# k and q turned by VectorE instead of TensorE in a pack attention with a softplus FFN behind it

## The chip, the cores and the metric

The kernel runs on one core of one Trainium2 chip. A core has five engines with instruction streams of their own: TensorE (PE in the profile; its weight loads are listed as PEld), VectorE (DVE), ScalarE (ACT), GpSimd (POOL) and SyncE (SP), whose queue issues nearly all DMAs here. The metric is the device time of one execution in microseconds: 802.89 us as the median of 3 runs, 802.77 to 803.67.

## What is computed

Eight batches of eight heads, 576 tokens, head size 64. Each head has 32 pack queries p. First the packs attend to the tokens, then the tokens attend to the packs, and the heads side by side (512 wide) go through a feed-forward layer of width 2048 with softplus. The weights of that layer come as 64-bit floats.

```
p_packed = softmax(p @ k.T / 8) @ v             # per batch and head: 32 x 64
a        = softmax(q @ p_packed.T / 8) @ p_packed   # 576 x 64
x        = heads of a side by side              # 4608 x 512
h        = x @ w_in                             # 4608 x 2048
out      = softplus(h) @ w_out                  # 4608 x 512
```

## The kernel before

**Groups and orientation.** The heads form two groups g of four (`HG`). For scores, the contraction over the head size has to lie on partitions, so k and q are needed turned: head size down, tokens across. `load` (L112) brings four heads of k, q or v as a tile of 96 partitions by 4 heads by 6 tokens by 64: each partition reads runs of six tokens, 1536 bytes. `transposed` (L223) turns one head: three TensorE transposes (L228) into a PSUM bank, two tokens of a run each, so that 128 partitions hold even tokens in the upper half and odd tokens in the lower, and one ScalarE copy (L234) to SBUF, the tile `T`. `scores1` and `scores2` (L241) multiply from there. The second scores are turned back by VectorE 32x32 transposes (L308, L332), which move data by blocks of 32 without TensorE.

The last attention product, by p_packed, is not computed as such: `make_m` (L447, bank `psm`) multiplies p_packed by a column chunk of w_in, and gemm1 takes the attention weights `at_h`, `at_l` against that.

**The FFN, in units.** A unit is one block of 128 of the 2048 columns for one batch, 16 units a batch. `gemm1` (L484) is twelve matmuls into two banks `ph` (a pool of two), three for each product since both sides are split into a high and a low part. The softplus is Abs, Exp and Ln on ScalarE (L506, L508, L509) into `e` and a max-and-add on VectorE (L511); POOL copies a rest of 64 tokens aside (L515), and VectorE splits `e` into `gh` and `gl` (L498, L499). `gemm2` (L522) of the unit two before follows: four tiles of 128 tokens, three matmuls each, into four banks `acc` that live through a batch. After an odd batch a fifth tile `acc_m` gathers the rests. `store` (L529) copies each result and writes it out.

**Stages.** In stage b the units of batch b run, and beside them, in steps of a generator, `attention` of batch b+1: a pacing number (`PACE`) says how many of its steps go between two gemm2 tiles. `make_m` stands behind the gemm2 of unit u for the chunk that starts at unit u+2: a chunk is 256 columns in batch 0, so every even unit has one, and 512 later. Stage 0 also runs `convert` (L148), another generator, paced by `CONV`: 32 pieces of the 64-bit weights, in the order i0 i1 o0 o1 i2 i3 o2 o3 and so on (i a block of w_in, o one of w_out). A piece is loaded into an `x` tile (L131), read twice by ScalarE (`m`, L173, and `r`, L177), worked on twice by VectorE (L179, L184) and added by POOL (L192), for i into `w_in_sb`; for o ScalarE and VectorE make `wo_h` (L211) and `wo_l` (L217) of it. From the ninth piece on there are two `x` tiles, so a load waits until the piece two before has been read.

**What sets the order.** TensorE's order is the order of the program text (`manual_schedule`). The orders of ScalarE, VectorE, POOL and SP are laid out when the kernel is built, by a scheduler that goes by its own idea of durations; on the chip they are fixed, and each engine runs its rows in order.

Of the kernel before, what the change touches and what calls it, by code (L numbers as in the profile page):

```python
# [9 lines left out]
F32 = mybir.dt.float32  # L10
# [16 lines left out]
def pack_attention_then_softplus_ffn(  # L27
# [10 lines left out]
    nc = tc.nc  # L38
    B, H, S, D = q.shape
    J = p.shape[2]  # L40
# [11 lines left out]
    LAG = 2  # L52
    MC = 512
    scale = 1.0 / math.sqrt(D)
# [23 lines left out]

    BG = P // J
    pT = const.tile([P, H, P], F32, name="pT")  # L80

# [10 lines left out]
    def load_pack(bg, queues):  # L92

        t = cv.tile([P, H, D], F32, tag="m", name=f"p_{bg}", bufs=1)
        for i in range(BG):
            queues[i % len(queues)].dma_start(
                t[i * J:(i + 1) * J], p[bg * BG + i].rearrange("h j d -> j h d")
            )
        return t

    def pack_transposed(bg, t):
        for o in range(0, H, HG):
            ps = bank(f"ppt_{bg}_{o}")
            for i in range(HG):
                nc.tensor.transpose(ps[:D, i * P:(i + 1) * P], t[:, o + i, :], ident)  # L105
            dst = pT[:, o:o + HG, :].rearrange("x h j -> x (h j)")
            nc.vector.tensor_copy(dst[:D], ps[:D])
            nc.scalar.copy(dst[D:], ps[:D])

    loaded = {}  # L110

    def load(nm, b, g):  # L112
        if b >= B:
            return
        t = ld.tile([NP, HG, SI, D], F32, tag="ld", name=f"{nm}_{b}_{g}")
        nc.sync.dma_start(
            t.rearrange("x h s d -> x h (s d)"),
            {"q": q, "k": k, "v": v}[nm][b, g * HG:(g + 1) * HG].rearrange(
                "h (x s) d -> x h (s d)", s=SI
            ),  # L120
        )
        loaded[nm, b, g] = t
# [99 lines left out]

    def transposed(nm, b, g, hh):  # L223

        src = loaded[nm, b, g]
        ps = bank(f"psT_{nm}_{b}_{g}_{hh}")
        for i in range(HS):
            nc.tensor.transpose(  # L228
                ps[:, i * NP:(i + 1) * NP],
                src[:, hh, 2 * i:2 * i + 2, :].rearrange("x s d -> x (s d)"),  # L230
                ident[:NP, :NP],
            )
        dst = work.tile([P, C], F32, tag="T", name=f"T_{nm}_{b}_{g}_{hh}", bufs=4)
        nc.scalar.copy(dst, ps[:, :C])  # L234
        return dst
# [98 lines left out]

    def attention(b):


        a1 = [work.tile([P, S], F32, tag="a1", name=f"a1_{b}_{g}") for g in range(G)]
        pp = [None] * G
        kT, qT = [], []  # L340
        for hh in range(HG):
            kT.append(transposed("k", b, 0, hh))
            yield
        load("q", b, 0)
# [4 lines left out]
        kT = [transposed("k", b, 1, 0)]  # L349
        yield  # L350
        z0 = softmax1_exp(b, 0, a1[0], nm)
        kT.append(transposed("k", b, 1, 1))
        yield
        rs0 = softmax1_sum(b, 0, z0)
        for hh in range(2, HG):
            kT.append(transposed("k", b, 1, hh))
            yield
        load("q", b, 1)
        for c in range(2):
# [12 lines left out]
        yield  # L372
        qT.append(transposed("q", b, 0, 0))
        yield
# [5 lines left out]
        yield  # L380
        qT.append(transposed("q", b, 0, 1))
        yield
# [3 lines left out]
        for hh in range(2, HG):  # L386
            qT.append(transposed("q", b, 0, hh))
            yield
# [28 lines left out]
        softmax2_div(b, 1, 1, a2n)  # L417
        yield

    def weights(b):  # L420
# [105 lines left out]

    outv = [out[b * S:(b + 1) * S, :].rearrange("(x s) e -> s x e", s=SI) for b in range(B)]

    def store(acc, pieces, nm):  # L529
        o = cv.tile([P, DM], F32, tag="x", name=f"o_{nm}", bufs=2)  # L530
        nc.vector.tensor_copy(o, acc)  # L531
        for row, b, col, n in pieces:
            while n:
                i, x = divmod(col, NP)
                m = min(n, NP - x)
                s = i % HS * 2 + i // HS
                nc.sync.dma_start(outv[b][s, x:x + m, :], o[row:row + m, :])
                row, col, n = row + m, col + m, n - m
# [142 lines left out]
```

## Time and profile before

| | |
|---|---|
| median of 3 runs | 802.89 us (802.77 to 803.67) |
| profiled execution | 803.84 us |
| its span, first to last instruction | 802.0 us |
| mean granted TensorE clock | 0.981 |
| packets under 512 bytes | 4864 of 38215 |
| k, q, v loads | 16 each, 576 KB, 4.6 to 4.8 us to landing |
| start of gemm1 in stages 0, 1, 2 | 44.9 (held to 49.5), 157.1, 243.3 us |

A row of a group gives the line, the engine, the operation, output and input tiles with shapes and a count; then the busy time in us, the mean of one in ns, and the idle time before such instructions with what ended it. A row by stretches gives the stretch, its length, then busy time and count of PE, PEld, VectorE, ScalarE and POOL, the granted clock, the DMA share and GB/s. A row of the timeline gives start, duration, engine, line and operation, and in brackets a wait and what ended it.

### The profile page before, as it was taken

To read this page: it belongs to the slowest core of one execution; us is meant where nothing else is said; L and a number is where in the kernel's file an instruction comes from. 1 tells how busy PE (TensorE), PEld (TensorE's weight loads), DVE (VectorE), ACT (ScalarE), POOL (GpSimd) and SP (SyncE) were. 2 spreads that over 40 slices of the span, in tenths; PEclk is the share of its full clock that TensorE was granted. 3 is DMA by queue.
4 is the path that set the end of the run, shared out by engine and by line. 5 is a ranking of instruction groups with operands and counts; after the bars stand their busy time and mean duration, and the time that the engine had idled before them with its cause. 6 is when DMAs were issued, how large, how long until landed. Compare 5 with 4: busy or idle time off the path is not lost.

```text
span 802.0 us, 14807 instructions
## 1 busy us (share of the span) xinstructions
PE 762.9 (95%) x5632; PEld 602.1 (75%) x5632; DVE 512.1 (64%) x1168; ACT 465.0 (58%) x1181; POOL 93.8 (12%) x166
## 2 busy tenths in 40 slices
PE   6368998999999999999999999999999999999997
PEld 4246666787788787887888777878778777878886
DVE  2787869864677447764677446765587546764554
ACT  5658877666554555675555465566556355555540
POOL 1414443100000000000000000000000000000010
PEclk9957999999999999999999999999999999999999
DMA  9975866022212112132212122122210210010002
GB/s 234 244 166 144 208 175 160 14 83 60 60 30 83 26 48 60 31 83 60 60 30 52 45 61 60 31 83 61 60 31 24 73 31 1 1 51 3 1 1 66
DMA packets 38215, 56.00 MB, mean 70 GB/s; under 512 B 4864, under 2 KB 31488, under 8 KB 38144
## 3 DMA queue, kind: packets, MB, share of 16 engines
q1 hardware_dynamic: 37600, 54.93, 26.7%
q8 instruction: 44, 0.72, 0.4%
q14 instruction: 27, 0.22, 0.1%
q10 hardware_dynamic: 544, 0.13, 0.1%
HBM read 45.61 MB, written 9.44 MB: 69 GB/s over the span
## 4 chain that ended last, share of the span: by engine, by line
PE 79%; ACT 0%; DVE 0%; issue 0%; ACTq 0%; DVEq 0%
PE acc L522 40%; PE ph L484 23%; PE acc_m L522 5%; PE psm L447 3%; PE ps L241 2%; PE psT_q L228 1%; PE psT_k L228 1%; PE psp L284 1%; PE psa L274 1%; PE psx L297 0%; PE ppt L105 0%; ACT e L509 0%; ACT e L508 0%; ACT e L506 0%; DVE o L531 0%; DVE o_m L531 0%
## 5 line engine op out<-in xcount | busy, mean ns | idle before, releaser
L511 DVE SCALAR_TENSOR_TENSOR e<-ph,e 128x288 f32<-128x288 f32 x256 | 114.5, 454 | 173.2 <-ACT e L509 170.2
L522 PE MATMUL acc<-wo_h,gh 128*128 128x512 f32 x512 | 214.5, 419 | 0.7 <-DVE o L531 0.7
L522 PE MATMUL acc<-wo_h,gl 128*128 128x512 f32 x512 | 201.4, 393 | 0.0
L522 PE MATMUL acc<-wo_l,gh 128*128 128x512 f32 x512 | 201.3, 393 | 0.0
L506 ACT ACTIVATE e<-ph 128x288 f32<-128x288 f32 x256 | 103.0, 403 | 166.4 <-PE ph L484 113.4
L484 PE MATMUL ph<-at_h,mh 128*128 128x288 f32 x512 | 161.0, 314 | 5.7 <-DVE e L511 4.1
L484 PE MATMUL ph<-at_l,mh 128*128 128x288 f32 x512 | 153.5, 300 | 4.3 <-DVE at_l L430 4.3
L484 PE MATMUL ph<-at_h,ml 128*128 128x288 f32 x512 | 153.4, 300 | 0.0
L484 PEld LDWEIGHTS ph<-at_h,mh 128*128 128x128 f32 x512 | 98.2, 192 | 41.9 <-DVE gl L499 14.5
L515 POOL COPY rest<-e 128x64 f32<-128x64 f32 x128 | 47.3, 370 | 609.5 <-DVE e L511 608.1
L522 PEld LDWEIGHTS acc<-wo_h,gh 128*128 128x128 f32 x512 | 96.4, 188 | 23.1 <-issue 9.8
L522 PEld LDWEIGHTS acc<-wo_h,gl 128*128 128x128 f32 x512 | 96.3, 188 | 21.7
L508 ACT ACTIVATE e<-e 128x288 f32<-128x288 f32 (+1 forms) x240 | 109.0, 454 | 3.6
L509 ACT ACTIVATE e<-e 128x288 f32<-128x288 f32 (+1 forms) x240 | 109.5, 456 | 1.9
L522 PEld LDWEIGHTS acc<-wo_l,gh 128*128 128x128 f32 x512 | 96.8, 189 | 9.8
L484 PEld LDWEIGHTS ph<-at_l,mh 128*128 128x128 f32 x512 | 98.4, 192 | 7.2 <-DVE at_l L430 5.0
L484 PEld LDWEIGHTS ph<-at_h,ml 128*128 128x128 f32 x512 | 98.4, 192 | 0.0
L499 DVE TENSOR_TENSOR gl<-e,gh 128x512 fp32r<-128x512 f32 x128 | 91.2, 712 | 6.4
L462 ACT CAST mh<-psm 128x512 fp32r<-128x512 f32 (+1 forms) x72 | 35.6, 541 | 43.8 <-PE psm L447 43.5
L498 DVE CAST gh<-e 128x512 fp32r<-128x512 f32 x128 | 54.7, 428 | 6.6 <-DVE e L511 0.5
L463 DVE TENSOR_TENSOR ml<-psm,mh 128x512 fp32r<-128x512 f32 (+1 forms) x72 | 42.8, 622 | 23.0 <-ACT mh L462 23.0
L447 PE MATMUL psm<-w_in_sb,pt 64*32 64x512 f32 (+1 forms) x576 | 41.1, 568 | 3.6 <-ACT T_q L234 2.3
(69 smaller groups left out, 796.9 us busy)
## 6 DMA issues: line engine op xcount, KB each, us to landing
k<-in_k SPq DMA_DIRECT2D x16, 576.0 KB, 4.6
v<-in_v SPq DMA_DIRECT2D x16, 576.0 KB, 4.6
q<-in_q SPq DMA_DIRECT2D x16, 576.0 KB, 4.8
x_i<-in_moe_w_in SPq DMA_DIRECT2D x32, 256.0 KB, 4.9
x_o<-in_moe_w_out SPq DMA_DIRECT2D x16, 512.0 KB, 4.4
out<-o SPq DMA_DIRECT2D x24, 192.0 KB, 2.4
out<-o SPq DMA_DIRECT2D x16, 128.0 KB, 2.3
out<-o SPq DMA_DIRECT2D x24, 64.0 KB, 2.2
```

The source lines that it names most:

```text
L447: nc.tensor.matmul(ps[hh * J:(hh + 1) * J, :n], res["pt"][g][o:o + D, hh * J:(hh + 1) * J], w_in_sb[o:o + D, hh, c * n:(c + 1) * n], start ...
L462: nc.scalar.copy(mh[:, cols], ps[:, :n])
L463: nc.vector.tensor_tensor(ml[:, cols], ps[:, :n], mh[:, cols].bitcast(F32), op=ALU.subtract)
L484: nc.tensor.matmul(ph[:, :C], x[:, ms], y[:, g, cs], start=(i == 0), stop=(i == 3 * G - 1),)
L498: nc.vector.tensor_copy(hi, x)
L499: nc.vector.tensor_tensor(lo, x, hi.bitcast(F32), op=ALU.subtract)
L506: nc.scalar.activation(es[c], hv[c], AF.Abs)
L508: nc.scalar.activation(x, x, AF.Exp, scale=-1.0)
L509: nc.scalar.activation(x, x, AF.Ln, bias=1.0)
L511: nc.vector.scalar_tensor_tensor(es[c], hv[c], 0.0, es[c], op0=ALU.max, op1=ALU.add)
L515: nc.gpsimd.tensor_copy(rest[:, rest_at(b, f), r:r + REST], e[:, NT * P:])
L522: nc.tensor.matmul(acc, x[:, cs], y[:, f, :], start=(first and i == 0), stop=(last and i == 2),)
```

## The change

From batch 1 on, k and q are loaded in runs of 32 of a token's 64 values (128 bytes), four DMAs a group, so that VectorE's 32x32 transposes can finish the turn: `quads` turns a load by two transposes of 128x576. `attention_next` is the order for those batches. v is read in runs of two tokens (512 bytes), since the order of tokens is now another, and `store` writes accordingly. Batch 0 keeps the TensorE transposes; its k and q lie in columns of `w_in_sb` that are not yet filled, and q is loaded ahead of the first blocks of w_out. p is packed for two batches at a time (four packs of 64 rows, not two of 128). Tiles `T` hold a whole group, two of them, and loads of k and q have a pool of two (`kq`).

```diff
-    ld = ctx.enter_context(tc.tile_pool(name="ld", bufs=2 * G))
+    ld = ctx.enter_context(tc.tile_pool(name="ld", bufs=G))
...
-    BG = P // J
-    pT = const.tile([P, H, P], F32, name="pT")
+    BG = 2
+    PW = BG * J
...
-        t = ld.tile([NP, HG, SI, D], F32, tag="ld", name=f"{nm}_{b}_{g}")
-        nc.sync.dma_start(
-            t.rearrange("x h s d -> x h (s d)"),
-            {"q": q, "k": k, "v": v}[nm][b, g * HG:(g + 1) * HG].rearrange(
-                "h (x s) d -> x h (s d)", s=SI
-            ),
-        )
+        src = {"q": q, "k": k, "v": v}[nm][b, g * HG:(g + 1) * HG]
+        if b < FIRST:
+            if nm == "v":
+                t = ld.tile([NP, HG, SI, D], F32, tag="v", name=f"{nm}_{b}_{g}")
+            else:
+                o = DFF - (["k", "q"].index(nm) * G + g + 1) * SI * D
+                t = w_in_sb[:NP, :, o:o + SI * D].rearrange("x h (s d) -> x h s d", d=D)
+            nc.sync.dma_start(
+                t.rearrange("x h s d -> x h (s d)"),
+                src.rearrange("h (x s) d -> x h (s d)", s=SI),
+            )
+        elif nm == "v":
+            t = ld.tile([NP, HG, SI, D], F32, tag="v", name=f"{nm}_{b}_{g}")
+            nc.sync.dma_start(
+                t.rearrange("x h (m c) d -> x (h m) (c d)", c=2),
+                src.rearrange("h (m x c) d -> x (h m) (c d)", x=NP, c=2),
+            )
+        else:
+            t = ld.tile([P, HG, C], F32, tag="kq", name=f"{nm}_{b}_{g}")
+            by_quad = src.rearrange("h (n x c) (e d) -> c e x (h n) d", x=Q, c=2, d=Q)
+            for i in range(P // Q):
+                nc.sync.dma_start(
+                    t[i * Q:(i + 1) * Q].rearrange("x h (n d) -> x (h n) d", d=Q),
+                    by_quad[i // 2, i % 2],
+                )
         loaded[nm, b, g] = t
...
-    def transposed(nm, b, g, hh):
+    def turned(nm, b, g):
+        return work.tile([P, HG, C], F32, tag="T", name=f"T_{nm}_{b}_{g}", bufs=2)
+
+    def quads(nm, b, g):
+        src, dst = loaded[nm, b, g], turned(nm, b, g)
+        for o in range(0, HG, 2):
+            nc.vector.transpose(
+                dst[:, o:o + 2, :].rearrange("x h n -> x (h n)"),
+                src[:, o:o + 2, :].rearrange("x h n -> x (h n)"),
+            )
+        return [dst[:, hh, :] for hh in range(HG)]
+
+    def transposed(nm, b, g, hh, into):
...
+    def attention_next(b):
+        a1 = [work.tile([P, S], F32, tag="a1", name=f"a1_{b}_{g}") for g in range(G)]
+        kT = [quads("k", b, 0)]
+        yield
+        load("q", b, 0)
+        kT.append(quads("k", b, 1))
+        yield
+        load("q", b, 1)
+        yield
+        for c in range(2):
+            scores1(b, 0, c, kT[0], a1[0])
+        yield
+        nm = softmax1_max(b, 0, a1[0])
+        yield
+        z0 = softmax1_exp(b, 0, a1[0], nm)
+        yield
+        for c in range(2):
+            scores1(b, 1, c, kT[1], a1[1])
+        qT = [quads("q", b, 0)]
+        yield
+        rs0 = softmax1_sum(b, 0, z0)
+        nm = softmax1_max(b, 1, a1[1])
+        yield
+        a1T = work.tile([NP, SI, P], F32, tag="a1T", name=f"a1T_{b}_0", bufs=1)
+        for c in range(2):
+            a1_transposed(b, 0, c, a1[0], a1T)
+            yield
+            if c == 0:
+                z1 = softmax1_exp(b, 1, a1[1], nm)
+        load("k", b + 1, 0)
+        yield
+        rs1 = softmax1_sum(b, 1, z1)
+        pp = [packed(b, 0, a1T, rs0)]
+        qT.append(quads("q", b, 1))
+        yield
+        load("k", b + 1, 1)
+        a1T = work.tile([NP, SI, P], F32, tag="a1T", name=f"a1T_{b}_1", bufs=1)
+        for c in range(2):
+            a1_transposed(b, 1, c, a1[1], a1T)
+            yield
+        res[b]["pt"].append(packed_transposed(b, 0, pp[0]))
+        yield
+        pp.append(packed(b, 1, a1T, rs1))
+        yield
+        load("v", b + 1, 0)
+        a2 = scores2(b, 0, 0, qT[0])
+        a2n = scores2(b, 0, 1, qT[0])
+        yield
+        res[b]["pt"].append(packed_transposed(b, 1, pp[1]))
+        yield
+        load("v", b + 1, 1)
...
+    def attention(b):
+        return attention_first(b) if b < FIRST else attention_next(b)
...
         load("k", 0, g)
     next(conv)
     load("v", 0, 0)
+    load("v", 0, 1)
+    for g in range(G):
+        load("q", 0, g)
     next(conv)
-    load("v", 0, 1)
     res = [{"pt": [], "aT": {}, "m": {}} for _ in range(B)]
 
     spare += [(ps_acc, "acc")] * NT + [(ps_m, "m")] * 2
```

The change moves rows on engines that it doesn't name, since the scheduler lays them out anew. Three places follow. In the names, a number behind the tile's own is one of the listing alone; x, m, r and t belong to the conversion, `e_6` is unit 6's softplus, and `psm_4` and `mh_4` its chunk for units 8 and 9.

ScalarE in stage 0, around the end of unit 6's softplus, before:

```order
L508 ACTIVATE e_6_1095<-e_6_1095 128x576
L234 COPY T_q_0_0_1109<-psT_q_0_0_1105 128x288
L509 ACTIVATE e_6_1095<-e_6_1095 128x576
L173 ACTIVATE m_1112<-x_i_1010 128x512
L177 ACTIVATE r_1114<-x_i_1010 128x512
L211 CAST wo_h<-t_1033 128x512
L275 COPY a1T_1_1128<-psa_1_0_1129 96x384
L462 CAST mh_4_0_1162<-psm_4_0_1152 128x256
```

and now, from the same Ln on:

```order
L622 ACTIVATE e_6_1067<-e_6_1067 128x576
L196 ACTIVATE m_753<-x_o_689 128x512
L200 ACTIVATE r_755<-x_o_689 128x512
L200 ACTIVATE r_824<-x_o_736 128x512
L196 ACTIVATE m_822<-x_o_736 128x512
L234 CAST wo_h<-t_757 128x512
L234 CAST wo_h<-t_826 128x512
L196 ACTIVATE m_883<-x_i_759 128x512
L200 ACTIVATE r_885<-x_i_759 128x512
L196 ACTIVATE m_909<-x_i_828 128x512
L200 ACTIVATE r_911<-x_i_828 128x512
L200 ACTIVATE r_973<-x_o_889 128x512
```

Before, x_i_1010 is block i10; i8 and i9, which `psm_4` multiplies by, stand ahead of e_5. Now x_o_689 and x_o_736 are o6 and o7, and x_i_759 and x_i_828 are i8 and i9: they stand between e_6 and `mh_4`, and their loads take the buffers that o6 and o7 free.

SP's queue at that place now, with the loads of the next batch but one among those of the weights:

```order
L154 DMA x_o_689<-in_moe_w_out 128x512
L154 DMA x_o_736<-in_moe_w_out 128x512
L141 DMA k_0_924<-in_k 32x36x32
L154 DMA x_i_759<-in_moe_w_in 64x4x128 x2
L154 DMA x_i_828<-in_moe_w_in 64x4x128 x2
L154 DMA x_o_889<-in_moe_w_out 128x512
```

The first quarter of a load of k for batch 2 (`k_0_924`) goes ahead of i8's.

VectorE from unit 1's softplus on, before:

```order
L511 SCALAR_TENSOR_TENSOR e_1_652<-ph_1_1_645,e_1_652 128x288
L179 TENSOR_SCALAR t_665<-m_661 128x512
L217 TENSOR_TENSOR wo_l<-t_617,wo_h 128x512
L184 SCALAR_TENSOR_TENSOR t_665<-m_661,t_665 128x512
L498 CAST gh_1_681<-e_1_652 128x512
L499 TENSOR_TENSOR gl_1_682<-e_1_652,gh_1_681 128x512
L179 TENSOR_SCALAR t_695<-m_691 128x512
```

and now:

```order
L624 SCALAR_TENSOR_TENSOR e_1_639<-ph_1_1_632,e_1_639 128x288
L611 CAST gh_1_667<-e_1_639 128x512
L612 TENSOR_TENSOR gl_1_668<-e_1_639,gh_1_667 128x512
L252 STREAM_TRANSPOSE T_k_0_574<-k_0_318 128x576 x2
L289 TENSOR_REDUCE m_1_0_719<-a_1_0_572 128x1
```

The conversions' rows are gone from this place, and the turn of batch 1's first k load stands behind unit 1's split. On TensorE the scores that need it stand ahead of gemm1 of unit 2; the second group's stand behind the first gemm2 tile of unit 3, and its turn behind unit 3's split.

More of the change, by code (lines that the diff above doesn't have):

```diff
@@ L77, in rest_at @@
         return f + NF if f < LAG and b // 2 % 2 else f
-    BG = P // J
-    pT = const.tile([P, H, P], F32, name="pT")
+    BG = 2
+    PW = BG * J
+    pT = const.tile([P, H, PW], F32, name="pT")
     spare = []
@@ L92, in load_pack @@
     def load_pack(bg, queues):
-        t = cv.tile([P, H, D], F32, tag="m", name=f"p_{bg}", bufs=1)
+        t = cv.tile([PW, H, D], F32, tag="m", name=f"p_{bg}", bufs=1)
         for i in range(BG):
@@ L232, in transposed @@
             )
-        dst = work.tile([P, C], F32, tag="T", name=f"T_{nm}_{b}_{g}_{hh}", bufs=4)
+        dst = into[:, hh, :]
         nc.scalar.copy(dst, ps[:, :C])
@@ L340, in attention @@
         kT, qT = [], []
+        kt = turned("k", b, 0)
         for hh in range(HG):
-            kT.append(transposed("k", b, 0, hh))
+            kT.append(transposed("k", b, 0, hh, kt))
             yield
-        load("q", b, 0)
         for c in range(2):
@@ L355, in attention @@
         for hh in range(2, HG):
-            kT.append(transposed("k", b, 1, hh))
+            kT.append(transposed("k", b, 1, hh, kt))
             yield
-        load("q", b, 1)
         for c in range(2):
@@ L372, in attention @@
         yield
-        qT.append(transposed("q", b, 0, 0))
+        qt = turned("q", b, 0)
+        qT.append(transposed("q", b, 0, 0, qt))
         yield
@@ L418, in attention @@
         yield
+    def attention_next(b):
[49 more added lines that the diff above has]
+        load("v", b + 1, 1)
+        softmax2_exp(b, 0, 0, a2)
+        yield
+        softmax2_div(b, 0, 0, a2)
+        yield
+        softmax2_exp(b, 0, 1, a2n)
+        yield
+        softmax2_div(b, 0, 1, a2n)
+        yield
+        a2 = scores2(b, 1, 0, qT[1])
+        a2n = scores2(b, 1, 1, qT[1])
+        yield
+        softmax2_exp(b, 1, 0, a2)
+        yield
+        softmax2_div(b, 1, 0, a2)
+        yield
+        softmax2_exp(b, 1, 1, a2n)
+        yield
+        softmax2_div(b, 1, 1, a2n)
+        yield
+    def attention(b):
+        return attention_first(b) if b < FIRST else attention_next(b)
     def weights(b):
@@ L525, in gemm2_tile, with rows @@
             )
-    outv = [out[b * S:(b + 1) * S, :].rearrange("(x s) e -> s x e", s=SI) for b in range(B)]
+    def rows(b, col, n):
+        o = out[b * S:(b + 1) * S, :]
+        c, t = divmod(col, C)
+        if b < FIRST:
+            i, x = divmod(t, NP)
+            n = min(n, NP - x)
+            return n, o.rearrange("(x s) e -> s x e", s=SI)[2 * i + c, x:x + n, :]
+        n = min(n, C - t)
+        return n, o.rearrange("(t c) e -> c t e", c=2)[c, t:t + n, :]
     def store(acc, pieces, nm):
@@ L533, in store @@
             while n:
[L534 to L537, printed above, removed]
+                m, dst = rows(b, col, n)
+                nc.sync.dma_start(dst, o[row:row + m, :])
                 row, col, n = row + m, col + m, n - m
```

30 lines of the change are left out of this document (18 added, 12 removed).

## Prediction

> **What bounds the kernel now.** I read the page's first two parts first, then the chain that ended last, then the busy time by stretches.
>
> ```profile
> span 802.0 us, 14807 instructions
> PE 762.9 (95%) x5632; PEld 602.1 (75%) x5632; DVE 512.1 (64%) x1168; ACT 465.0 (58%) x1181; POOL 93.8 (12%) x166
> PEclk9957999999999999999999999999999999999999
> PE 79%; ACT 0%; DVE 0%; issue 0%; ACTq 0%; DVEq 0%
> core 0: us, PE busy (x) PEld busy (x) DVE busy (x) ACT busy (x) POOL busy (x), PEclk, DMA share, GB/s
> 49.50:157.10 107.60, 97.00 (x709) 71.80 (x709) 87.48 (x192) 81.68 (x174) 38.53 (x38) 0.90 0.54 141
> 354.00:440.00 86.00, 86.00 (x658) 68.82 (x654) 55.98 (x133) 50.29 (x135) 5.92 (x16) 1.00 0.21 55
> ```
>
> TensorE is busy 95% of the span, and the chain names hardly anything else. But the two stretches differ. From 354 to 440 us (a steady stage, sixteen units) PE is busy 86.00 of 86.00 us, VectorE 56 and ScalarE 50: there each microsecond taken off PE is one off the span. From 49.5 to 157.1 us (stage 0, the same sixteen units beside the conversion of the weights) PE is busy 97.0 of 107.6 us at clock 0.90, with VectorE at 87.5 and ScalarE at 81.7. That stretch is 21.6 us longer than a steady one, and all three engines are close to full. So the change is worth one thing in stages 1 to 6 and another in stage 0 and before it.
>
> **Stages 1 to 6: TensorE's transposes go.** One head of k or q is three small transposes put between the FFN's matmuls:
>
> ```profile
> 376.14 0.39 PE L522 MATMUL acc<-wo_h,gl 128*128 128x512 f32 x1
> 376.37 0.41 PE L228 MATMUL psT_q<-ident,q 96*128 96x96 f32 x3
> 376.57 0.48 PE L522 MATMUL acc<-wo_h,gh 128*128 128x512 f32 x1
> 376.88 0.40 PE L522 MATMUL acc<-wo_l,gh 128*128 128x512 f32 x1
> L228 PE MATMUL psT_k<-ident,k 96*128 96x96 f32 x192 | 28.3, 269 | 1.1 <-DMA k<-in_k 0.6 <-ACT T_k L234 0.5
> ```
>
> Durations overlap in the pipeline, so the busy time of a group is not its price; starts are. From the acc at 376.14 to the acc at 376.88, two starts later, it is 0.74 us with the three transposes between; without them two accs take 2 x 0.23 = 0.46. The price is 0.28 us a head. A batch has 16 heads of k and q (192 transposes of k over 8 batches are 8 groups of three each): 16 x 0.28 = 4.5 us. Six stages bound by PE give 6 x 4.5 = 27 us. The packs' smaller tiles (four of 64 rows for two of 128) add two sets of eight half-width transposes, some 1 us in all: **-26 us**.
>
> What VectorE takes over is not on that path while it has room. The form it gets, 128x576, has no row; its nearest is the same operation on half as many columns:
>
> ```profile
> L332 DVE STREAM_TRANSPOSE aT<-a 128x288 f32<-128x288 f32 x32 | 15.1, 471 | 0.2
> L234 ACT COPY T_k<-psT_k 128x288 f32<-128x288 f32 x64 | 24.9, 396 | 27.3 <-PE psT_k L228 26.4
> ```
>
> Bounds: 0.47 us if twice the columns cost nothing, 0.94 if they cost double. I take 0.9: eight a batch are 7.2 us more on VectorE, 56 + 7 = 63 of 82 us, and ScalarE loses 16 copies of 0.4 us. In the steady stages the turns stand ahead of need (k's next batch from unit 8 on), so I cost them at nothing. The cover is VectorE's idle quarter; if it were gone they would cost up to 7 us a stage.
>
> The loads become 4608 runs of 128 bytes. No run of 128 bytes is in the trace; 256 bytes are, when a pack is loaded:
>
> ```profile
> q1 hardware_dynamic: 1088, 0.26, 28.5%
> p<-in_p SPq DMA_DIRECT2D x4, 64.0 KB, 2.0
> ```
>
> That window is 4 us: 0.285 x 16 x 4 us / 1088 = 17 ns of one engine a packet. From below a packet of half the bytes takes half, 8 ns; from above, if the latency of the four issues were all packet time (2.0 us x 16 / 256), 125 ns. I take 17: 4608 x 17 ns / 16 = 4.9 us a load beside 4.8 now, and four loads a batch against 82 us are hidden. The Trainium skill, "DMA: Bandwidth & Descriptors", section "Specifications", states 512 bytes as the least transfer for line rate, with a read-modify-write below it. By that rule a 128-byte run could cost twice what the 256-byte rows give, 10 us a load, which the steady stages would still hide; no run here shows it yet, as 256 bytes lie below the limit too and stand beside no longer packet.
>
> **Ahead of stage 0.** q's two loads of batch 0 come before the weights. Now PE waits for them:
>
> ```profile
> 29.97 0.71 PE L228 MATMUL psT_q<-ident,q 96*128 96x96 f32 x3 [10.30 <-DMA q<-in_q]
> 49.47 0.61 PE L484 MATMUL ph<-at_l,mh 128*128 128x288 f32 x1 [3.98 <-DVE at_l L430]
> ```
>
> The 10.3 us wait goes, but gemm1 still needs the same ten conversions ahead of it in ScalarE's and VectorE's orders, and what these engines do in that wait comes after it instead. Bounds: 0 and -10. I take **-3**, near the lower, as the next late thing is the chain that ends in the 3.98 us wait for at_l.
>
> **Stage 0: the conversions lose their lead.** This term decides. The static order of ScalarE, shown above, has six conversions between e_6 and e_7 where it had two, and none in units 0 to 3 (one to three a unit before). PE's order is by hand: psm of unit 6 stands behind unit 4's gemm2 and needs weight blocks i8 and i9, and only two x buffers are left, so i8 and i9 cannot be loaded until o6 and o7 have been read. Before, i8 and i9 were converted ahead of e_5. The prices:
>
> ```profile
> x_i<-in_moe_w_in SPq DMA_DIRECT2D x16, 256.0 KB, 4.0
> L173 ACT ACTIVATE m<-x_i 128x512 f32<-128x512 f32 x16 | 10.7, 671 | 0.0
> L177 ACT ACTIVATE r<-x_i 128x512 int32<-128x512 uint32 x16 | 10.7, 668 | 0.0
> L179 DVE TENSOR_SCALAR t<-m 128x512 int32<-128x512 int32 x32 | 15.3, 479 | 8.0 <-ACT m L173 6.7 <-ACT e L506 0.9
> L184 DVE SCALAR_TENSOR_TENSOR t<-m,t 128x512 int32<-128x512 int32 x32 | 23.7, 740 | 0.4
> L192 POOL TENSOR_TENSOR w_in_sb<-t,r 128x512 int32<-128x512 int32 x16 | 22.5, 1409 | 52.5 <-DVE t L184 14.1 <-ACT a L261 12.5 <-ACT e L506 11.2
> L506 ACT ACTIVATE e<-ph 128x288 f32<-128x288 f32 x256 | 103.0, 403 | 166.4 <-PE ph L484 113.4 <-issue 31.5 <-DVE m L316 16.1
> L508 ACT ACTIVATE e<-e 128x576 f32<-128x576 f32 x16 | 10.9, 683 | 0.2
> L509 ACT ACTIVATE e<-e 128x576 f32<-128x576 f32 x16 | 10.9, 682 | 0.1
> 92.25 0.41 PE L484 MATMUL ph<-at_h,mh 128*128 128x288 f32 x1
> 93.95 0.39 PE L522 MATMUL acc<-wo_h,gh 128*128 128x512 f32 x1
> 97.44 0.42 PE L447 MATMUL psm<-w_in_sb,pt 64*32 64x256 f32 x4
> ```
>
> Unit 6: from the end of gemm1, ScalarE takes 0.40 + 0.68 + 0.68 = 1.8 us for the softplus, 1.34 for o6; then i8's load runs 4.0, i8 and i9 are read in 2 x 1.34, i9's two VectorE steps take 1.2 and POOL's add 1.4: together 12.4 us. PE has a gemm2 to do meanwhile, 93.95 to 97.44 with its inserts, about 3.1 without those that go. It waits 9.3 us. Unit 10 has the same rows: 9.3. In unit 4 only the second block's load waits, for o5 between Exp and Ln: 0.4 + 0.7 + 1.3 + 4.0 + 1.3 + 1.2 + 1.4 = 10.3 less 3.4, 7 us. In units 8 and 12 the loads are there and two reads stand behind the softplus: 1.8 + 2.7 + 1.2 + 1.4 = 7.1 less 3.1, 4 each. Sum 34 us. Ahead of it, scores of batch 1 stand in PE's order ahead of gemm1 of unit 2, and behind the first gemm2 tile of unit 3; both need turns that VectorE's order puts behind that unit's split:
>
> ```profile
> L511 DVE SCALAR_TENSOR_TENSOR e<-ph,e 128x288 f32<-128x288 f32 x256 | 114.5, 454 | 173.2 <-ACT e L509 170.2 <-ACT e L508 2.7
> L498 DVE CAST gh<-e 128x512 fp32r<-128x512 f32 x128 | 54.7, 428 | 6.6 <-DVE e L511 0.5
> L499 DVE TENSOR_TENSOR gl<-e,gh 128x512 fp32r<-128x512 f32 x128 | 91.2, 712 | 6.4
> ```
>
> Softplus 1.8, twice 0.45, 0.43, 0.71 and two turns of 0.9 are 5.6 us after gemm1. At unit 2 PE would have waited 2.2 us for gemm1's banks anyway, so 3.4 is new; at unit 3 three matmuls lie beside it and three tiles come after: 4.6. Together 8. Against this stand today's own waits ahead of psm:
>
> ```profile
> L447 PE MATMUL psm<-w_in_sb,pt 64*32 64x256 f32 x128 | 10.6, 453 | 3.6 <-ACT T_q L234 2.3 <-ACT a1T L275 0.7 <-DVE a L308 0.3
> 109.67 0.64 PE L447 MATMUL psm<-w_in_sb,pt 64*32 64x256 f32 x8
> 112.31 0.83 PE L447 MATMUL psm<-w_in_sb,pt 64*32 64x256 f32 x8 [2.00 <-ACT T_q L234]
> 113.48 0.44 PE L484 MATMUL ph<-at_l,mh 128*128 128x288 f32 x1
> 113.72 0.44 PE L484 MATMUL ph<-at_h,ml 128*128 128x288 f32 x1
> ```
>
> These 3.6 us go, and the transposes' own 4.5 us count in the 9 of 16 units where PE doesn't wait: -2.5. Stage 0: 34 + 8 - 3.6 - 2.5 = **+36 us**. Two things I leave out as of one size: the units without conversions run lighter (up to -8 us of the 21.6), and the clock. After the 2 us wait above, gemm1's matmuls start 0.24 us apart, though these pass in 0.14 at full clock (92.25 to 93.95 for twelve), so each of the seven waits could add about 1.4 us, +10.
>
> The sum: 803.84 (the profiled execution's own time, 802.0 of span and 1.8 around it) - 3 + 36 - 26 = 810.8. That execution lies 0.95 us above the median of 802.89, so 809.9; with a k load of the next batch but one in the queue ahead of i8's (a quarter of 4.9 us), **811 us**, 1% slower.
>
> **Rivals.**
>
> *The conversions keep pace.* PE's clear 26 us arrive, stage 0 shrinks by its own 4.5 and the start by 3: 803 - 33.5 = 770 us. For it: ScalarE and VectorE in stage 0 lose 16 copies and have 20 us of room. Against it: the orders are fixed, and a load behind two reads cannot start early. Anything under +28 us in stage 0 still ends faster, with 780 to 800. Chance 0.24 together.
>
> *The two cancel.* Stage 0 longer by 27 to 31: 801 to 805. Chance 0.05.
>
> *Short runs hold up the weights.* In stage 0, six loads of 128-byte runs go through the queue that brings x, two of them among x_o6 to x_i11. If a packet takes 35 ns, a load takes 10 us in place of 4.9, and the three waits with a load inside grow by up to 5 us each: 811 + 15 = 826. From about 60 ns a packet (17 us a load, 70 us a stage) the steady stages would be bound by it as well, and the time passes 840. Against: the 17 ns above. Chance 0.12, of which 0.04 over 840.
>
> *The clock falls at each wait.* Waits of 4 to 9 us, each followed by slow matmuls as after 112.31, and nothing given back by the light units: 811 + 10 = 821. The Trainium skill, "TensorE: Matmul & The Clock Gate", Part 1, states that the clock falls to half after an idle window of about 3.4 us; the trace shows it after a shorter one. Chance 0.2; my own forecast keeps 0.39.
>
> **The numbers.** Forecast 811, its own range 803 to 819. The range for 8 in 10 takes in half of the faster case and all but the worst of the slower ones: 782 to 836. Differences under 0.2% (1.6 us) cannot be told from none. Faster 0.24, same 0.05, slower 0.71.
>
> **What would show it.** In the steady stages PE stays busy throughout, and each lasts 4.5 us less: else the first term is wrong. In stage 0, PE's waits ahead of psm of units 4, 6, 8, 10 and 12 should name POOL, with 7 to 9 us at 4, 6 and 10, and its waits for the first scores should name VectorE's turn. If stage 0 lasts under 130 us the forecast falls; if the waits name the k or q load, the packet price did.

## The result, and the profile after

The changed kernel takes 836.17 us (median of 4 runs, 835.87 to 838.75) against 803.28 us for the kernel before on the same chips: ratio 1.0415, 95% interval 1.0391 to 1.0438. It is 4.2% slower. From the page of the changed kernel, its first two parts and the chain that ended last:

```profile
span 834.5 us, 14191 instructions
PE 734.6 (88%) x5312; PEld 580.9 (70%) x5312; DVE 543.5 (65%) x1228; ACT 434.1 (52%) x1073; POOL 89.5 (11%) x166
PEclk9557788768999999999999999999999999999999
PE 78%; DVE 9%; DMA 5%; ACT 4%; issue 2%; POOL 2%; SPq 0%; DVEq 0%; POOLq 0%; ACTq 0%
```

TensorE has 28 us less to do and a span that is 32.5 us longer. VectorE, DMA, ScalarE and POOL now stand in the chain. The clock row says where: in the second to tenth slice of 40, which are the start and stage 0. By stretches, for the changed kernel (unit 1 of stage 0 up to stage 1, and all that follows):

```profile
58.50:215.40 156.90, 92.61 (x643) 70.78 (x643) 93.89 (x193) 76.73 (x150) 34.53 (x37) 0.77 0.43 98
215.40:834.50 619.10, 613.58 (x4397) 491.33 (x4396) 414.52 (x956) 324.79 (x852) 41.13 (x113) 1.00 0.21 45
```

and the same two stretches of the kernel before:

```profile
57.00:157.10 100.10, 90.52 (x680) 67.68 (x676) 83.47 (x181) 77.09 (x165) 37.25 (x37) 0.93 0.54 144
157.10:802.00 644.90, 639.75 (x4676) 514.12 (x4676) 394.97 (x909) 354.28 (x945) 41.74 (x113) 1.00 0.17 45
```

The start is 1.5 us later (58.5 for 57.0), stage 0 from unit 1 on takes 156.9 us for 100.1, and the rest 619.1 for 644.9. These are +1.5, +56.8 and -25.8, together +32.5. (Here and in the table further down, "stage 0" is counted from the start of unit 1's gemm1, and the start and unit 0 lie ahead of it.) In stage 0 TensorE is busy for about the same time as before, 92.6 us for 90.5. What grew is its idle time, from 10 to 64 us. Its waits over the whole of the changed kernel, in us, with how many and the longest:

```profile
PE psm L560 <- POOL w_in_sb L215: 51.8, 5, 15.8
PE ph L597 <- DVE at_l L543: 12.0, 1, 12.0
PE ps L276 <- DVE T_k L252: 8.9, 2, 4.8
PE ph L597 <- ACT at_h L542: 5.9, 1, 5.9
```

Five waits of `make_m` for the add of a weight block account for 51.8 us. TensorE's timeline shows them one by one (start, duration, work, and in brackets the wait before it):

```profile
100.79 1.11 PE L560 MATMUL psm<-w_in_sb,pt 64*32 64x256 f32 x16 [9.48 <-POOL w_in_sb L215]
126.34 1.11 PE L560 MATMUL psm<-w_in_sb,pt 64*32 64x256 f32 x16 [12.13 <-POOL w_in_sb L215]
149.18 1.11 PE L560 MATMUL psm<-w_in_sb,pt 64*32 64x256 f32 x16 [9.97 <-POOL w_in_sb L215]
177.23 1.11 PE L560 MATMUL psm<-w_in_sb,pt 64*32 64x256 f32 x16 [15.85 <-POOL w_in_sb L215]
197.14 0.74 PE L560 MATMUL psm<-w_in_sb,pt 64*32 64x256 f32 x16 [4.41 <-POOL w_in_sb L215]
```

They stand in units 4, 6, 8, 10 and 12 of TensorE's order, behind the gemm2 of the unit two before, and each is for the chunk that starts two units on. That the first of them is a matter of order and not of a transfer is seen in these views. SP's queue issued the load of o4 at

```profile
48.68 0.66 SPq L154 DMA_DIRECT2D x_o<-in_moe_w_out  x1
```

and a load of w_out lands 5.6 us after its issue (median up to 170 us). ScalarE read o4 35 us after the issue, and no wait for its load is shown:

```profile
83.76 0.68 ACT L196 ACTIVATE m<-x_o 128x512 f32<-128x512 f32 x1
```

So o4 lay in its buffer for some 30 us; its row on ScalarE came only behind unit 3's softplus. The next loads in the order, those of i6 and i7, wait for the buffers of o4 and o5. SP issued i6 when o4 had been read, 28 us later than in the kernel before, whose row for i6 stands second:

```profile
85.02 6.74 SPq L154 DMA_DIRECT2D x_i<-in_moe_w_in  x4
57.09 1.26 SPq L131 DMA_DIRECT2D x_i<-in_moe_w_in  x2
```

From there each later load waits for a buffer that an earlier, late conversion holds.

What VectorE took over, and what a load of 128-byte runs costs, are now rows too. The turns of k, as a group (those of q are alike, 0.77 us each):

```profile
L252 DVE STREAM_TRANSPOSE T_k<-k 128x576 f32<-128x576 f32 x28 | 21.1, 758 | 0.0
```

and the DMA engines in a stretch of 4.9 us with one load of q in it, of the changed kernel (packets, MB, share of the sixteen engines):

```profile
q1 hardware_dynamic: 4672, 0.59, 76.3%
```

0.763 x 16 x 4.9 us / 4672 is 12.8 ns of one engine a packet, and 3.7 us of all sixteen for the load. The same bytes in 1536-byte runs, in a stretch of 5 us of the kernel before:

```profile
q1 hardware_dynamic: 400, 0.59, 44.5%
```

That is 2.2 us of all sixteen.

### The profile page after: what moved, and what is told of

It is laid out like the page before. It is cut to its first block, busy times and chain, and to the rows that moved or that the text cites. A ratio compares the mean times of both kernels' runs of the same rounds, so it can differ in the third digit from the quotient of the medians.

```text
span 834.5 us, 14191 instructions
## 1 busy us (share of the span) xinstructions
PE 734.6 (88%) x5312; PEld 580.9 (70%) x5312; DVE 543.5 (65%) x1228; ACT 434.1 (52%) x1073; POOL 89.5 (11%) x166
## 4 chain that ended last, share of the span: by engine, by line
PE 78%; DVE 9%; DMA 5%; ACT 4%; issue 2%; POOL 2%; SPq 0%; DVEq 0%; POOLq 0%; ACTq 0%
PE acc L635 39%; PE ph L597 25%; PE acc_m L635 4%; PE psm L560 4%; DMA x_o<-in_moe_w_out 2%; PE ps L276 2%; DVE t L207 2%; DMA x_i<-in_moe_w_in 1%; PE psp L319 1%; POOL t L215 1%; DVE t L202 1%; PE psa L309 1%; ACT m L196 1%; DMA out<-o 1%; DVE e L624 1%
## 5 line engine op out<-in xcount | busy, mean ns | idle before, releaser
L635 PE MATMUL acc<-wo_h,gh 128*128 128x512 f32 x512 | 208.5, 407 | 0.0
L597 PE MATMUL ph<-at_l,mh 128*128 128x288 f32 x512 | 155.7, 304 | 12.0 <-DVE at_l L543 12.0
L597 PE MATMUL ph<-at_h,ml 128*128 128x288 f32 x512 | 155.8, 304 | 0.0
L597 PEld LDWEIGHTS ph<-at_h,mh 128*128 128x128 f32 x512 | 100.4, 196 | 47.0 <-issue 16.4
L628 POOL COPY rest<-e 128x64 f32<-128x64 f32 x128 | 46.5, 363 | 621.4 <-DVE e L624 592.4
L597 PEld LDWEIGHTS ph<-at_l,mh 128*128 128x128 f32 x512 | 100.7, 197 | 15.5 <-DVE at_l L543 12.4
L597 PEld LDWEIGHTS ph<-at_h,ml 128*128 128x128 f32 x512 | 100.6, 196 | 0.0
L612 DVE TENSOR_TENSOR gl<-e,gh 128x512 fp32r<-128x512 f32 x128 | 87.9, 686 | 6.6 <-DVE gh L611 0.5
L560 PE MATMUL psm<-w_in_sb,pt 64*32 64x512 f32 (+1 forms) x576 | 38.7, 595 | 51.8 <-POOL w_in_sb L215 51.8
```

Of the source, the lines that this page charges most:

```text
L560: nc.tensor.matmul(ps[hh * J:(hh + 1) * J, :n], res["pt"][g][o:o + D, hh * J:(hh + 1) * J], w_in_sb[o:o + D, hh, c * n:(c + 1) * n], start ...
L597: nc.tensor.matmul(ph[:, :C], x[:, ms], y[:, g, cs], start=(i == 0), stop=(i == 3 * G - 1),)
L612: nc.vector.tensor_tensor(lo, x, hi.bitcast(F32), op=ALU.subtract)
L628: nc.gpsimd.tensor_copy(rest[:, rest_at(b, f), r:r + REST], e[:, NT * P:])
L635: nc.tensor.matmul(acc, x[:, cs], y[:, f, :], start=(first and i == 0), stop=(last and i == 2),)
```

## The experiments

Two theories stood against each other for stage 0. By the first, the conversions' place in the fixed orders is the cause: their lead is gone, so `make_m` waits. By the second, the short runs, or the queue they go through, hold up the weights themselves. The table gives for each kernel the time, and from its trace when gemm1 of unit 1 starts, how long stage 0 takes from there, and what follows up to the end of the span; all in us.

| kernel | time | unit 1 | stage 0 | rest |
|---|---|---|---|---|
| before | 803.28 | 57.0 | 100.1 | 644.9 |
| changed | 836.17 | 58.5 | 156.9 | 619.1 |
| q_late | 831.57 | 56.4 | 153.5 | 619.9 |
| long_runs | 808.86 | 58.7 | 129.5 | 618.9 |
| before_128 | 814.02 | 57.4 | 109.6 | 645.2 |
| loads_from_act | 808.20 | 62.3 | 106.8 | 635.8 |
| sp_priority | 827.75 | 59.7 | 141.3 | 624.0 |
| stage0_from_act | 798.66 | 56.9 | 119.0 | 621.0 |
| stage0_from_act_later | 802.75 | 56.2 | 119.7 | 625.1 |
| stage0_from_pool | 795.75 | 59.4 | 113.7 | 619.9 |
| k1_by_tensore | 803.04 | 56.1 | 120.5 | 624.7 |
| k1_by_tensore_act | 788.88 | 63.3 | 105.2 | 619.1 |
| k1_by_tensore_act_w | 789.52 | 63.3 | 105.0 | 619.3 |
| k1_by_tensore_pool_w | 792.47 | 56.4 | 109.5 | 625.1 |

q_late, long_runs, before_128, sp_priority and stage0_from_pool were run once; the kernel before took 801 to 809 us beside these runs, so differences of a few microseconds between single runs carry nothing. The columns are from one trace of each kernel; there I read only what a named wait explains.

**q_late: the early q undone.**

```diff
-    for g in range(G):
-        load("q", 0, g)
     next(conv)
...
+        load("q", b, 0)
         for c in range(2):
             scores1(b, 0, c, kT, a1[0])
...
+        load("q", b, 1)
```

> The changed kernel with batch 0's q loaded as late as before (after the first group's k has been turned), everything else kept. Main theory (the weight conversions stand too late in the fixed orders of stage 0, because their loads stand behind the loads of k and q in SP's queue as the scheduler laid it out): the conversions stand per unit as in the changed kernel, so stage 0 from unit 1 on keeps its 157 us and the five waits of 52 us for POOL; the time is 834 to 842. Rival (the early q displaces the first weights at the start and the conversions never catch up): 790 to 815. The start itself: if the early q is worth what was forecast, gemm1 flows 3 us later than in the changed kernel.

831.57 us, 2.4 us under the main theory's range. The waits for POOL stay:

```profile
PE psm L562 <- POOL w_in_sb L215: 51.5, 5, 15.8
```

The early q is not what cost stage 0. And it did not help the start: without it unit 1 starts 2.1 us earlier, not 3 us later.

**long_runs: the same quarters in 1152-byte runs.**

```diff
-            by_quad = src.rearrange("h (n x c) (e d) -> c e x (h n) d", x=Q, c=2, d=Q)
+            by_part = src.rearrange("h s d -> h (s d)").rearrange("h (i x n) -> i x h n", i=4, x=Q)
```

> The changed kernel with the loads of k and q from batch 1 on read in runs of 1152 bytes into the same 32-partition quarters, so four DMAs a load as before but 128 descriptors of 1152 bytes in place of 1152 of 128; the order of values in the tile is another, so this leaves out the right arrangement of k and q. Main theory: what counts is where the conversions stand; in this kernel's ScalarE order they stand 1, 1, 2, 2, 4, 1, 1, 1, 5 in units 2 to 10, a lead in part, so stage 0 is 15 to 35 us shorter than in the changed kernel: 800 to 820. Rival (the short runs themselves are slow and hold up the weights): they are gone entirely and stage 0 is back at 107 us: 775 to 785.

808.86 us, in the main theory's range, with stage 0 shorter by 27 us but not back:

```profile
PE psm L560 <- POOL w_in_sb L215: 33.6, 5, 11.5
```

The order moved with the change (the scheduler laid the conversions a unit or two earlier), and the waits followed. The run does not separate the two theories for the 27 us, since runs and order changed together. But 33.6 us of waits without any 128-byte run of k or q say that such runs are not needed for the waits.

**before_128: short runs alone.** The kernel before, with k and q in halves of 32 values:

```diff
+            for hh in range(HG):
+                for e in range(2):
+                    ds = slice(e * 32, (e + 1) * 32)
+                    nc.sync.dma_start(
+                        t[:, hh, :, ds], src[hh, :, ds].rearrange("(x s) d -> x s d", s=SI)
+                    )
```

> The kernel before with one part of the change alone: k and q from batch 1 on are loaded in runs of 128 bytes (two halves of a token's 64 values, eight DMAs a load), into the old tile, and TensorE goes on turning them. ScalarE's order keeps the conversions' lead (2, 2, 1, 3, 1, 2 in units 1 to 6). Main theory: a load of 128-byte runs costs about 5 us of the DMA engines as its packets of 17 ns say, which is hidden: 800 to 808. Rival (short runs crowd out the weights in stage 0): stage 0 grows by 10 us or more: 813 to 835.

814.02 us, and what is more lies in stage 0: 109.6 us for 100.1, the rest as before. That is the rival's figure; my own expectation of no cost missed. The 9.5 us went in small pieces. The longest waits of stage 0 (the first of them was 4.1 us in the kernel before, the second not there):

```profile
PE ph L491 <- DVE e L518: 7.2, 5, 2.8
PE psm L454 <- POOL w_in_sb L199: 3.0, 1, 3.0
```

This kernel issues eight DMAs a load where the changed one issues four, and its ScalarE order is not quite that of the kernel before either. So 9.5 us is what short runs, their eight issues and this order cost together beside the weights, in one run of this kernel; how much of it is the transfers stays open, and so does what they cost in the changed kernel.

**loads_from_act: the same loads from another queue.**

```diff
-                nc.sync.dma_start(
+                nc.scalar.dma_start(
                     t[i * Q:(i + 1) * Q].rearrange("x h (n d) -> x (h n) d", d=Q),
```

> The changed kernel with the 128-byte loads of k and q issued from ScalarE's queue and not SP's; the same descriptors, the same DMA engines. ScalarE's order then has the conversions at 1, 2, 2, 1, 2, 2, 2, 2, 1, 2, 2, 1, 2 in units 0 to 12, as before the change. Main theory: the waits for POOL go from 52 us to under 10, stage 0 from unit 1 on takes 100 to 112 us, the steady stages keep their 26 us: 775 to 795. Rival (128-byte runs slow the weights' transfers or adds): the waits for POOL stay above 25 us: 810 to 830. What could spoil both: if an issue holds ScalarE for 0.9 us, as SP's rows show for SP, 128 issues put up to 16 us a stage on ScalarE, and gemm1 waits for the softplus.

808.20 us, ratio to before 1.0064 (1.004 to 1.0088). Stage 0 takes 106.8 us, 50 less than in the changed kernel, with the same 128-byte runs. Both the order and SP's queue are other here, so the 50 us belong to the two together. No wait for POOL is left among TensorE's waits, which now begin with

```profile
PE ph L597 <- DVE e L624: 24.6, 15, 3.0
PE psa L309 <- ACT a L296: 12.6, 1, 12.6
```

This is the main theory's figure for stage 0. The total missed its range, and the expectation had named what could do that: ScalarE's issues now stand among the softplus rows that gemm1 waits for. The rest takes 635.8 us for 619.1; gemm1's waits for `e` behind stage 0 come to 9.4 us, where the changed kernel shows none. The start takes 3.8 us more. Two issues took ScalarE's queue

```profile
97.20 5.35 ACTq L141 DMA_DIRECT2D k<-in_k  x2
```

5.35 us at one place, where the shortest single ones take 0.32 us, and ScalarE's next row came 5.8 us late.

**sp_priority: the orders alone.** Queue and sizes of the loads as in the changed kernel; only the scheduler's priority of the conversions, their loads with them, is raised:

```diff
                     while cdue >= 1:
-                        next(conv, None)
+                        with tc.high_priority(offset=2000):
+                            next(conv, None)
```

> The changed kernel with all loads on SP's queue as they were, and the conversions beside stage 0 given a higher priority in the scheduler: they stand 0, 0, 0, 2, 3, 2, 2, 6, 2, 1, 4 in units 0 to 10, ahead of the changed kernel's 0, 0, 0, 1, 3, 0, 5, 1, 2, 0, 6. The loads, their queue and their sizes stay, only the order moves. Main theory: the waits for POOL ahead of units 6 and 10 shrink by half or more, 10 to 25 us of the 52, and the time is 810 to 828. Rival (the queue and the short runs set stage 0, not the order): within 5 us of the changed kernel's 836.

827.75 us, at the upper end of the main theory's range. The waits for POOL fall by 44 us with nothing but the orders changed, which is the main theory. But another wait comes in their place:

```profile
PE ps L276 <- DVE T_q L252: 32.4, 2, 18.0
PE psm L560 <- POOL w_in_sb L215: 8.1, 2, 6.9
```

The turns of q for batch 1 now come late. SP's order moved too: the quarters of q's two loads stand singly or by twos among loads of weights that wait for a buffer, and go out from 94.9 to 160.4 us, where the changed kernel issued them from 67.0 to 69.8 and from 91.9 to 95.7. So in this order the one gains much of what the other loses: stage 0 is 15.6 us shorter, not 44.

**stage0_from_act, stage0_from_act_later, stage0_from_pool: only stage 0's loads moved.** In all three batch 0's q is loaded late again, as in q_late.

```diff
-                nc.sync.dma_start(
+                (nc.scalar if b == 1 and nm == "q" or b == 2 and nm == "k" else nc.sync).dma_start(
```

> The changed kernel with only the loads of q of batch 1 and of k of batch 2, those that stage 0 issues beside the weights, taken from SP's queue and given to ScalarE's; all later ones stay with SP, and batch 0's q is loaded as late as before. The conversions stand 0, 3, 2, 1, 2, 2, 2, 2, 1, 2, 2, 1, 2 in units 0 to 12. Main theory (stage 0 was lost to the conversions' place, and ScalarE's issues cost what the run with all loads from ScalarE lost in stages 1 to 6): start as in the run with the late q (unit 1 at 56.4 us), stage 0 from unit 1 on 100 to 110 us, the rest 614 us as in the changed kernel: 775 to 792, faster than both kernels. Rival (the 128-byte loads themselves take stage 0's time): stage 0 above 125 us, 800 or more.

> The run before it in this list, with the first scores of batch 1 two steps later for each group in the order of TensorE, so that VectorE's turns need not be done within a unit. If the turns' place costs what the waits of TensorE for T_k say (8.9 us in the changed kernel), it is 4 to 9 us below that run: 768 to 786. If these waits only hide behind others, within 2 us of it.

> As the first of this list, with k and q of batch 1 and k of batch 2 issued by GpSimd and not by ScalarE. The conversions stand 1, 2, 1, 2, 2, 2, 2, 0, 2, 2, 2, 0, 3 in units 0 to 12. Main theory: order restored, so stage 0 as there, if issuing 4608 descriptors a load costs GpSimd less than 5 us; each us beyond holds up the adds that psm waits for: 778 to 805. Rival (128-byte runs): 800 or more with waits for DMA, not for POOL.

The first takes 798.66 us, ratio 0.9929 (0.9902 to 0.9956): below both kernels, with the rest back at 621 us, but above its forecast of 775 to 792. Stage 0 takes 119.0 us where 100 to 110 were forecast, and unit 2 alone lasts from 62.6 to 85.2 us. q's loads wait for tiles that k's turns must free, and that wait now stands on ScalarE's queue: a copy behind it came 2.2 us late. More came from the weights. SP issued o4 only at 64.1 us, though i4 and i5 had been read from the two buffers by 46.5 us; the trace puts SP's wait down to q's load on the other queue. ScalarE, which has the reads of o4 and o5 ahead of unit 2's softplus, then waited 4.9 us for o4 and 3.6 for o5:

```profile
SPq L154 <- DMA q<-in_q: 17.8, 1, 17.8
69.53 0.67 ACT L196 ACTIVATE m<-x_o 128x512 f32<-128x512 f32 x1 [4.86 <-DMA x_o<-in_moe_w_out]
```

TensorE's longest waits in stage 0:

```profile
PE ph L599 <- DVE e L626: 19.6, 8, 7.7
PE psm L562 <- ACT a L285: 6.9, 1, 6.9
```

With the scores two steps later it is no better, 802.75 us (0.9962, 0.9943 to 0.9981), which neither of the two expectations had; a wait of 14.3 us for the same copy ahead of psm takes the place. Issued from GpSimd (with batch 1's k as well) it takes 795.75 us in one run, within its forecast.

**k1_by_tensore and its variants: batch 1's k turned as before.** Its k goes into columns of w_in_sb that batch 0 has done with, so q's loads find free tiles. Its v is read as in batch 0, batch 0's q is loaded late, and k of batch 2 comes from ScalarE's queue (from GpSimd's in the last variant):

```diff
-        if b < FIRST:
+        if b < FIRST or b == FIRST and nm != "q":
...
-        return attention_first(b) if b < FIRST else attention_next(b)
+        return (attention_first if b < FIRST else attention_mixed if b == FIRST else attention_next)(b)
```

where `attention_mixed` has the first half of `attention_first` and the second of `attention_next`.

> The changed kernel with batch 1's k and v loaded and k turned by TensorE as before the change (k lies in columns of w_in_sb that batch 0 has used); only its q is turned by VectorE, and q's loads find free buffers and wait for nothing. k of batch 2 is loaded from ScalarE's queue, all else from SP's; batch 0's q is loaded late. The conversions stand 1, 0, 0, 0, 5, 3, 2, 2, 3, 2, 1, 2, 1 in units 0 to 12, so the lead is back from unit 5 on. Main theory: no wait of TensorE for T_k by VectorE, waits for POOL only ahead of unit 4 or 6 and under 15 us, stage 0 from unit 1 on 105 to 120, the rest 614: 780 to 798. Rival (the 128-byte loads beside the weights set stage 0): above 120 us, over 798.

> As the run before it, with q of batch 1 from ScalarE's queue too; the conversions stand 2, 1, 3, 1, 2, 2, 2, 2, 1, 2, 1, 1, 2. Since its loads wait for no buffer, ScalarE's issues hold nothing up for long, but they stand ahead of gemm1 and share the DMA engines with the first weights. Main theory: stage 0 from unit 1 on 100 to 110 us, the start 0 to 5 us later than with the late q: 777 to 792, the lowest of all. If the queue was not what cost the lead but the sizes of the loads, no better than the run before it.

> The run k1_by_tensore_act with one wait added: a small copy by GpSimd writes the two tiles for batch 1's q from at_h of batch 0 first, so that ScalarE issues their loads only when gemm1 of stage 0 is about to start, and the first weights have the DMA engines alone. If that run's start (unit 1 at 63.3 us in place of 56.4) was lost to the early loads of q, 5 to 7 us come back: 780 to 785. If ScalarE's issues cost the same wherever they stand, 787 to 792.

> As the run before it, with q of batch 1 and k of batch 2 issued by GpSimd. The conversions stand 1, 1, 1, 3, 2, 2, 1, 2, 3, 1, 2, 1, 2 in units 0 to 12. ScalarE is relieved; GpSimd has the adds of the conversions and the issues on one queue. Main theory: within 4 us of the run before it, 778 to 789; if issuing holds GpSimd for several us a load, waits for POOL ahead of psm come back and it is 790 to 800.

k1_by_tensore, with q on SP's queue, is at 803.04 us (0.998, 0.9959 to 1.0001), above its forecast of 780 to 798 and, with stage 0 at 120.5 us, just where the rival had it. The longest wait of its stage 0 is for POOL and not for a load of k or q,

```profile
PE psm L642 <- POOL w_in_sb L215: 11.8, 1, 11.8
```

ahead of unit 4's psm, whose conversions stand after the gap that its order has in units 1 to 3. With q from ScalarE's queue the wait for POOL is 2.5 us, and it takes **788.88 us, ratio 0.9797 (0.9761 to 0.9833)**: the lowest median of all, 2% below the kernel before, with stage 0 at 105 us and the whole gain of the steady stages. At the start it loses 6.3 us against the kernel before, and 6.9 against q_late, where 0 to 5 were expected. The added wait was to bring these back, and the total did not move: 789.52 us, unit 1 at 63.3 us again, the figure expected if the issues cost the same wherever they stand. The trace shows where the gain went. gemm1 of unit 0 does start 3.0 us earlier, at 47.1 us for 50.2, but q's last issues now stand at the end of unit 0's softplus, a copy of k's turn behind them came 2.1 us late, and psm of unit 0 waits for it:

```profile
57.64 2.77 ACTq L143 DMA_DIRECT2D q<-in_q  x3
60.99 1.08 PE L644 MATMUL psm<-w_in_sb,pt 64*32 64x256 f32 x8 [3.59 <-ACT T_k L271]
```

From GpSimd unit 1 starts at 56.4 us, but stage 0 (109.5 us) and what follows (625.1) lose it again: 792.47 us (0.9857, 0.9834 to 0.9881), in the range expected if issuing holds GpSimd up, though no wait for POOL is among TensorE's longest.

## Why the prediction was right and wrong

The direction was right: slower. The time, 836.17 us, lies just past the upper end of 782 to 836 and 25 us above the forecast of 811. The mechanism was the one forecast; the step that failed is the size of one term, the waits for the weights in stage 0, put at 34 us and measured at 51.8.

**Stages 1 to 6** were forecast at -26 us; all after stage 0 is 25.8 us shorter, at 99% busy. That three transposes on TensorE are worth the distance of starts between neighbours (0.28 us), and not their busy time, is borne out: the sum is within 0.2 us. The turn on VectorE was taken at 0.9 us and measures 0.76; it cost nothing there, as forecast.

**Waits for the first scores** were forecast at 8 us new; TensorE waits 8.9 us for T_k, 4.8 at unit 2 and 4.1 at unit 3.

**Waits for the weights**: the term that failed. Its five parts against the trace:

| unit | 4 | 6 | 8 | 10 | 12 | sum |
|---|---|---|---|---|---|---|
| forecast | 7 | 9.3 | 4 | 9.3 | 4 | 34 |
| measured | 9.48 | 12.13 | 9.97 | 15.85 | 4.41 | 51.8 |

I summed each engine's own rows for the block in question and left out what else stands in those orders. ScalarE's timeline in the changed kernel shows two kinds of it:

```profile
96.97 0.66 ACT L196 ACTIVATE m<-x_i 128x512 f32<-128x512 f32 x1 [2.66 <-DVE t L207]
117.31 0.62 ACT L234 CAST wo_h<-t 128x512 fp32r<-128x512 f32 x1 [0.99 <-POOL t L215]
120.04 0.62 ACT L234 CAST wo_h<-t 128x512 fp32r<-128x512 f32 x1 [2.11 <-POOL t L215]
143.55 0.67 ACT L196 ACTIVATE m<-x_i 128x512 f32<-128x512 f32 x1 [2.63 <-issue]
166.07 0.62 ACT L234 CAST wo_h<-t 128x512 fp32r<-128x512 f32 x1 [0.68 <-POOL t L215]
169.46 0.62 ACT L234 CAST wo_h<-t 128x512 fp32r<-128x512 f32 x1 [2.76 <-POOL t L215]
173.43 0.66 ACT L196 ACTIVATE m<-x_i 128x512 f32<-128x512 f32 x1 [2.22 <-issue]
```

The first kind: in units 6 and 10 the casts of o6 and o7 (o10 and o11) stand ahead of the reads of the i blocks and wait for POOL. SP issued these i loads from

```profile
114.26 3.34 SPq L154 DMA_DIRECT2D x_i<-in_moe_w_in  x4
160.78 5.90 SPq L154 DMA_DIRECT2D x_i<-in_moe_w_in  x4
```

on, and such a load lands in 4.1 us, so the first was there at about 118.4 and 164.9 us; ScalarE read it at

```profile
120.56 0.66 ACT L196 ACTIVATE m<-x_i 128x512 f32<-128x512 f32 x1
169.98 0.66 ACT L196 ACTIVATE m<-x_i 128x512 f32<-128x512 f32 x1
```

about 2 and 5 us later, by an estimate from these rows. The order printed ahead of the prediction had the two casts in plain sight. (The prediction also reads "none in units 0 to 3" for the conversions, where o4's reads stand behind unit 3's softplus; none of the five parts rests on that.) The second kind: in units 4, 8 and 10 the second block's `m` waits 2.2 to 2.7 us; there is one `m` tile, and it is free only when VectorE has done both steps of the first block. In unit 4 the row names that step, L207. In unit 8 VectorE's rows for the two blocks stand among the softmax of the tokens and a turn of k:

```profile
142.78 0.69 DVE L207 SCALAR_TENSOR_TENSOR t<-m,t 128x512 int32<-128x512 int32 x1
143.77 1.14 DVE L361 TENSOR_SCALAR z<-z 128x9 f32<-128x9 f32 x1
144.83 0.76 DVE L252 STREAM_TRANSPOSE T_k<-k 128x576 f32<-128x576 f32 x1
147.03 0.69 DVE L207 SCALAR_TENSOR_TENSOR t<-m,t 128x512 int32<-128x512 int32 x1
```

**The start** was forecast at -3 us and is +1.5. The 10.3 us wait for q went, but two others grew: gemm1 waits 5.9 us for at_h and 12.0 for at_l (0.9 and 4.0 before). The prediction named that chain as next late and did not work it out.

Stage 0 is 20.8 us above its forecast (56.8 for 36), 17.8 of it in the waits for the weights, and the start 4.5: these are the 25 us by which 811 was missed.

**The terms left out as of one size**, lighter units and the clock, did about cancel: with 51.8 and 8.9 us in their places the forecast's sum for stage 0 is 54.6, and 56.8 were measured. TensorE's busy time in stage 0 rose by 2.1 us with 37 matmuls fewer, at clock 0.77. After a wait gemm1 runs 0.24 us a matmul, at a granted clock of 0.50 (101.8 to 104.8 us), and the distance is back at full speed within 3 to 5 us of work:

```profile
102.23 0.44 PE L597 MATMUL ph<-at_l,mh 128*128 128x288 f32 x1
102.47 0.44 PE L597 MATMUL ph<-at_h,ml 128*128 128x288 f32 x1
105.60 0.39 PE L635 MATMUL acc<-wo_h,gl 128*128 128x512 f32 x1
105.83 0.40 PE L635 MATMUL acc<-wo_h,gh 128*128 128x512 f32 x1
```

That the clock falls at each wait was a rival at 821. It happens: twelve matmuls at 0.24 us take 1.2 us more than at 0.14, near the 1.4 given for a wait, and seven of these are 8.4 us, less than the 20.8 by which stage 0 missed. The Trainium skill, "TensorE: Matmul & The Clock Gate", Part 1, puts the half clock after an idle window of about 3.4 us; the waits of 4 to 16 us here agree, while the kernel before showed it after a wait of 2.0 us already (granted clock 1.00 up to 112.3 us, 0.54 from there to 116).

**Short runs** were a rival at 826 if a packet took 35 ns. A packet takes 12.8 ns, less than the 17 forecast, and not the double that the prediction weighed beside it. The Trainium skill, "DMA: Bandwidth & Descriptors", section "Specifications", sets 512 bytes as the least for line rate; here 128-byte runs need 3.7 us of the sixteen engines where 1536-byte runs need 2.2, so the trace agrees in direction, at a factor of 1.7. In the run with short runs alone stage 0 grew by 9.5 us, where the forecast had 1.2 us for them (a quarter of a load). How much of the changed kernel's 56.8 us is theirs no run separates; its long waits in stage 0 are for POOL and for the turns, and none of them is for a load of k or q.

What is shown: the 52 us of waits come from the lost lead. o4 lay ready for 30 us, the waits stay with the early q undone, and they fall by 44 us when only the orders are changed. What is argued: that the lead with the same loads would give back all of stage 0. The run that had it, loads_from_act, also took the loads off SP's queue; the run that changed the orders alone got 15.6 us back, as q's loads then came late. What stays open: by what property of these loads the scheduler laid the conversions late, since both another queue and longer runs move them; and why SP waited for q's load in stage0_from_act.

## What to carry to other kernels

A change to the loads of one part can move the rows of another on every engine whose order a scheduler lays out; compare the orders, and look first for a group whose lead over the rows that use its result has gone. When you sum up such a wait, take every row that stands ahead on the in-order engines, and every tile with a single buffer, not only the rows of the chain you follow. A gain that holds in the steady stages (here 26 us) is worth keeping, and the stage that lost it worth treating by itself: with batch 1's k left as it was and its q on another queue, the same idea gives 788.88 us against 804.38 for the kernel before beside it.

## What the runs showed of the hardware

- A load of 4608 runs of 128 bytes takes 12.8 ns of a DMA engine a packet, 3.7 us for 576 KB on sixteen engines, against 2.2 us in 1536-byte runs: 1.7 times the engine time, and hidden in the steady stages.
- Issuing such DMAs is not free for the engine that does it: with all of them on ScalarE's queue the stages after stage 0 take 16.7 us more (635.8 for 619.1), and an issue that takes long, 5.35 us for two of them, holds up the row behind it by 5.8 us.
- VectorE turns 128x576 in 0.76 us, where 128x288 takes 0.47: less than double.
